# Phases of the convolution kernels as integers: a multiplication and two shifts instead of rounding and subtracting, integers read by ScalarE, and another order of the sums on TensorE

## The chip, the cores and the metric

The kernel runs on one core of a Trainium2 chip. The metric is device time in microseconds (us); the median of three runs of the kernel before is 2972.42 us (2969.39 to 2973.13). A profiled execution gives times of single instructions.

The engines are named as in the profile: PE (TensorE, matrix products; PEld its weight loads), DVE (VectorE, elementwise), ACT (ScalarE, functions such as exp and sin), POOL (GpSimd) and SP (which starts DMA transfers here). Each works off its own queue in order and waits at semaphores for the others. L431 means line 431 of the kernel.

## What is computed

Four layers on a sequence of 2048 positions and 640 channels: convolution layer, attention layer, and both again, each behind a layer norm and with a residual. Both convolution layers use the same kernel K, made from complex exponentials, which is what the change touches:

```python
def _A_ref(u, A_re, A_im, B_re, B_im, C_re, C_im, log_dt, Dskip):
    dt = jnp.exp(log_dt)[:, None]
    A = A_re + 1j * A_im
    ...
    logdA = dt * A
    dB = dt * Bc
    l = jnp.arange(L)
    P = jnp.exp(logdA[:, :, None] * l[None, None, :])
    K = jnp.einsum("dn,dnl,dn->dl", Cc, P, dB).real
    ...                       # y = causal convolution of u with K by FFT
    return y + u * Dskip

x = x + _A_ref(_layernorm(x), ...)
x = x + _B_ref(_layernorm(x), ...)    # attention, 32 query heads, one key/value head
x = x + _A_ref(_layernorm(x), ...)
x = x + _B_ref(_layernorm(x), ...)
```

For each of 640 channels d and 2048 positions l, K sums 128 complex exponentials. A position is split as l = 32 i + s with 64 values of i and 32 of s, so that an exponential is the product of one that depends on i and one that depends on s, and the sum over the 128 states is a small matrix product for each channel.

## The kernel before

The program runs in stages: generation of the kernels (`kgen`, up to about 300 us of the trace), spectra of the kernels, the first convolution layer, attention, the second convolution layer, attention. Only `_kgen` is touched.

`_kgen` first makes tables of three-part bf16 numbers (`ta`, `tb`, `tm`) from the parameters. Then 20 **units** of 32 channels each (16 channels times 2 parities) pass through a pipeline; a unit u needs:

- **phases**, two tiles h = 0, 1 of 128 x 1024. `phase_first(u, h)` has PE multiply a table by a constant grid `kg` into the PSUM tile `ph` (one buffer of two banks): the phase in turns, up to some sixteen of them. `phase(u, h)` has DVE take the fraction in [-0.5, 0.5]: `magic_round` (L241) rounds to whole turns into `r`, and L431 subtracts, into `f` (four buffers). Each reads `ph` from PSUM.
- **trig(u, h)** on ACT: Abs of `f` into `fa` (L444), sine of `f` (L445), cosine as sine of a quarter turn minus `fa` (L446). h = 0 gives C1 and S1, h = 1 gives C2 and S2. Two POOL memsets set the first column of C1 and S1.
- **sizes(u, k)** on PE, k = 0, 1, 2: the exponents of the magnitudes, into the PSUM tile `pe` with two buffers; **exps(u, k)** on ACT: exp of these (L462 for k = 0 and 1, into M1; L464 for k = 2, into M2).
- **products(u, k)** on DVE, k = 0, 1, 2, two operations each: magnitude by cosine into E1R (L472, L473), magnitude by sine in place into M1 (L476, L478), and C2 and S2 by M2 (L480, L481).
- **sums(u, ds)** on PE (L491): for each slice d of eight, small matmuls of E1R by C2 and M1 by S2 into the PSUM tile `pk`.
- **store(u)**: ACT copies `pk` out (L500) and SP stores it.

The order on PE, ACT and DVE is written out by hand (`manual_schedule`); the loop counts u from 0 to 22 and works on several units in one pass: in pass u the sizes, exponentials and trig of unit u, the phases of unit u + 1, the products of unit u - 1, the sums of unit u - 2, and the store of unit u - 3. Even and odd passes differ on ACT, so that sine and exp, which need different function tables, come in long runs: an even pass does both trigs and then the exponentials, an odd pass the exponentials and then both trigs. Passes 5 to 12 also hold the statistics of two tokens' tiles for the layer norm on DVE (L685, L687). Behind the last unit the weights of the transform (`wf`, L607) are loaded into space that the tables leave, and the spectra begin (L629).

The attention layers hold a DVE path, `power`, that is not touched: it turns scores from PSUM to int32 (L1356) and cuts the integers by bitwise operations (L1359, L1360).

Of the kernel before, what the change touches and what calls it, by code (L numbers as in the profile page):

```python
# [11 lines left out]
F32 = mybir.dt.float32  # L12
F32R = mybir.dt.float32r
BF16 = mybir.dt.bfloat16
I32 = mybir.dt.int32
AF = mybir.ActivationFunctionType
ALU = mybir.AluOpType
# [4 lines left out]
P = 128  # L22
# [6 lines left out]
TWO_PI = 2.0 * math.pi  # L29
# [170 lines left out]
class Net:  # L200
# [159 lines left out]
    def _kgen(self, ctx):  # L360
        tc, nc, ins = self.tc, self.nc, self.ins
# [33 lines left out]
        bp = ctx.enter_context(tc.tile_pool(name="kgb", bufs=2, reuse_waits="tile"))  # L395
# [1 line left out]

        units = [(q, r, q * 256 + 16 * r, 128, 128) for q in range(2) for r in range(8)]
        units += [(2, r, 512 + 16 * r, 64, 64) for r in range(4)]
        C1, S1, C2, S2, M1, M2, E1R, F, PH, PE_, PK, KST = ({} for _ in range(12))  # L400
        KST[0, 0] = bp.tile([P, 64, 32], F32, tag="kst", bufs=2, name="kst00")

        def big(tag, u, x, bufs=2):
            return bp.tile([P, 16, 2, x], F32, tag=tag, bufs=bufs, name=f"{tag}_{u}")

        def swap(a):
            return a.rearrange("p d a s -> p a d s")
# [8 lines left out]
        def phase_first(u, h):  # L416

            pp = PH[u, h] = kp.tile([P, 1024], F32, tag="ph", bufs=1, name=f"ph{u}{h}")
            src, col, rows = ((tb, 0, 48), (ta, 512, 96))[h]
            for par in range(2):  # L420
                nc.tensor.matmul(pp[:, 512 * par : 512 * par + 512], grp(src, u, par, rows),
                                 kg[0:rows, col : col + 512], start=True, stop=True)

        def phase(u, h):
            if (u, h) not in PH:
                phase_first(u, h)
            pp = PH.pop((u, h))
            r = bp.tile([P, 1024], BF16, tag="r", bufs=2, name=f"r{u}{h}")
            self.magic_round(r, pp)
            F[u, h] = bp.tile([P, 1024], F32, tag="f", bufs=4, name=f"f{u}{h}")  # L430
            nc.vector.tensor_tensor(F[u, h], pp, r, ALU.subtract)  # L431

        def trig(u, h):
            if h == 0:
                C1[u], S1[u] = big("c1", u, 33), big("s1", u, 33)
                nc.gpsimd.memset(C1[u][:, :, :, 0:1], 1.0)
                nc.gpsimd.memset(S1[u][:, :, :, 0:1], 0.0)
                s, c = swap(S1[u])[:, :, :, 1:33], swap(C1[u])[:, :, :, 1:33]
            else:
                C2[u], S2[u] = big("c2", u, 32, 3), big("s2", u, 32, 3)  # L440
                s, c = swap(S2[u]), swap(C2[u])
            f = F.pop((u, h))
            fa = bp.tile([P, 1024], F32, tag="fa", bufs=1, name=f"fa{u}{h}")
            nc.scalar.activation(fa, f, AF.Abs)  # L444
            nc.scalar.activation(s, f.rearrange("p (a d s) -> p a d s", a=2, d=16), AF.Sin, scale=TWO_PI)  # L445
            nc.scalar.activation(c, fa.rearrange("p (a d s) -> p a d s", a=2, d=16), AF.Sin,  # L446
                                 scale=-TWO_PI, bias=self.halfpi)

        def sizes(u, k):

# [15 lines left out]
        def products(u, k):  # L466

            tt = nc.vector.tensor_tensor
            if k == 0:
                E1R[u] = big("e1r", u, 64, 2)  # L470
                er, m1, c1 = (fl(a[u]) for a in (E1R, M1, C1))
                tt(er[:, :, 32:64], m1[:, :, 32:64], c1[:, :, 0:32], ALU.mult)  # L472
                tt(er[:, :, 0:32], m1[:, :, 0:32], c1[:, :, 32:0:-1], ALU.mult)  # L473
            elif k == 1:
                m1, s1 = (fl(a.pop(u)) for a in (dict(M1), S1))
                nc.vector.scalar_tensor_tensor(m1[:, :, 32:64], m1[:, :, 32:64], -1.0, s1[:, :, 0:32],  # L476
                                               op0=ALU.mult, op1=ALU.mult)
                tt(m1[:, :, 0:32], m1[:, :, 0:32], s1[:, :, 32:0:-1], ALU.mult)  # L478
            else:
                tt(C2[u], C2[u], M2[u], ALU.mult)  # L480
                tt(S2[u], S2[u], M2[u], ALU.mult)  # L481

        def sums(u, ds):

            if u not in PK:
                PK[u] = kp.tile([P, 512], F32, tag="pk", bufs=2, name=f"pk{u}")
            for d in ds:
                for e, c, first in ((E1R, C2, True), (M1, S2, False)):
                    for s in range(4):
                        dd, par = 8 * (s % 2) + d, s // 2  # L490
                        nc.tensor.matmul(PK[u][32 * s : 32 * s + 32, 64 * d : 64 * d + 64],  # L491
                                         c[u][:, dd, par], e[u][:, dd, par], start=first, stop=not first)

        def store(u):
            q, r, _, _, run = units[u]
            h, g = divmod(r, 4)
            if g == 0 and u > 0:
                KST[q, h] = bp.tile([P, 64, 32], F32, tag="kst", bufs=2, name=f"kst{q}{h}")
            kst = KST[q, h]
            nc.scalar.activation(kst[:, :, 8 * g : 8 * g + 8], PK[u].rearrange("p (d i) -> p i d", d=8), AF.Copy)  # L500
            if g == 3:
                for s in range(4):
                    par, dh = s // 2, s % 2
                    kd = self.kd[2 * q + par] if run == 128 else self.kd[4]
                    c0 = run // 2 * dh + 32 * h + (0 if run == 128 else 64 * par)
                    for jh in range(2):
                        dst = kd[64 * jh : 64 * jh + 64].rearrange("i (t d) -> t i d", d=DC)[:, :, c0 : c0 + 32]
                        nc.sync.dma_start(dst, kst[32 * s + 16 * jh : 32 * s + 16 * jh + 16])
            if r == 2 and q > 0:
                for c in (2 * q - 2, 2 * q - 1):  # L510
                    self.skip(c, self.kd[c, 0:1, 0:DC])
# [4 lines left out]
        with tc.manual_schedule(engines=engines):  # L516
            for h in range(2):
                phase(0, h)
            for u in range(n + 3):
                now, nxt, prod, tot = u < n, u + 1 < n, 0 < u <= n, 2 <= u < n + 2  # L520
                odd = u % 2 == 1
                if u >= 3:
                    store(u - 3)
                if now and not odd:
                    trig(u, 0)
                if prod:
                    products(u - 1, 0)
                if now:
                    sizes(u, 0)
                    if odd:  # L530
                        exps(u, 0)
                if nxt:
                    phase_first(u + 1, 0)
                if tot:
                    sums(u - 2, range(0, 2))
                if now:
                    sizes(u, 1)
                    if odd:
                        exps(u, 1)
                if tot:  # L540
                    sums(u - 2, range(2, 3))
                if nxt:
                    phase(u + 1, 0)
                if now and odd:
                    sizes(u, 2)
                    exps(u, 2)
                if prod:
                    products(u - 1, 1)
                if now:
                    trig(u, 0 if odd else 1)  # L550
                if tot:
                    sums(u - 2, range(3, 5))
                if nxt:
                    phase(u + 1, 1)
                if prod:
                    products(u - 1, 2)
                if tot:
                    sums(u - 2, range(5, 7))
                if now:
                    if odd:  # L560
                        trig(u, 1)
                    else:
                        exps(u, 0)
                        sizes(u, 2)
                        exps(u, 1)
                        exps(u, 2)
                if tot:
                    sums(u - 2, range(7, 8))
                if u == 0:
                    self.load_x()  # L570
                    nc.sync.dma_start(self.ident, ins["c_id"])
                if 5 <= u < 13:
                    self.stats(u - 5)
                for t in {n: range(8, 12), n + 1: range(12, 16)}.get(u, ()):
                    self.stats(t)
                if u == n:
                    early.close()
                    self.conv_weights(nc.sync)
# [1054 lines left out]
```

## Time and profile before

| | us |
|---|---|
| median of three runs | 2972.42 |
| lowest, highest | 2969.39, 2973.13 |
| profiled execution, whole | 2973.82 |
| its span, first to last instruction | 2971.8 |
| mean granted TensorE clock | 0.952 |

A row of a timeline gives the start in us from the span's start, the time in us, engine, line, operation, the tile written and those read, sizes, how many instructions are merged, and in brackets how long the engine sat idle before and what released it. A row of the groups gives line, engine, operation, shapes and count, then the busy time in us and the mean of one in ns, then idle time before them and its releasers. Consecutive DVE and ACT instructions overlap a little in their records, so the distance from start to start is the better measure of what one costs in a sequence.

### The profile page before, as it was taken

The page shows a single profiled execution, that of the slowest core. Times are in us where ns is not written, and L with a number is a line of the kernel's source. Part 1 is how long each engine was busy: PE and PEld are TensorE (multiplying, and loading weights), DVE is VectorE, ACT ScalarE, POOL GpSimd, SP SyncE. Part 2 cuts the span into 40 slices and gives each one's busy share as a digit, 9 for nine tenths or more (in the row PEclk, how much of TensorE's full clock was granted, in tenths as well). Part 3 has the DMA queues.
Part 4 walks back from the last instruction along what each step waited for, and adds up shares of the span by engine and source line. Part 5 has one row for each costly group of instructions (what it writes and reads, how often), then busy time and mean ns, then how long its engine had stood idle before and what let it go on. Part 6 is the DMA issues. An engine that isn't in the chain of part 4 may idle for free. (4 is left out here: it accounts for less than half of the span.)

```text
span 2971.8 us, 71403 instructions
## 1 busy us (share of the span) xinstructions
PE 2720.8 (92%) x29916; PEld 1563.3 (53%) x29916; DVE 2375.0 (80%) x2820; ACT 2397.1 (81%) x3065; POOL 293.1 (10%) x514
## 2 busy tenths in 40 slices
PE   2776989898899999999999999898999999999999
PEld 0333978775344444444444688773444444444444
DVE  7999899943678888888888699826788888878885
ACT  5888243444899999999999734337999999999997
POOL 0000001100201011010101011001111110101101
PEclk9655999998999999999999999898999999999999
DMA  6113555533211111111111255231111211211211
GB/s 146 35 17 99 172 183 114 119 122 104 84 36 33 35 33 36 35 35 37 31 36 34 92 114 126 87 127 54 34 34 35 55 33 37 51 35 33 54 32 31
DMA packets 156101, 196.30 MB, mean 66 GB/s; under 512 B 66221, under 2 KB 123533, under 8 KB 152149
## 3 DMA queue, kind: packets, MB, share of 16 engines
q1 hardware_dynamic: 119704, 141.90, 16.2%
q0 software_dynamic: 33776, 48.08, 8.0%
q8 instruction: 239, 3.92, 0.5%
q10 hardware_dynamic: 2288, 1.64, 0.2%
q14 instruction: 94, 0.76, 0.1%
HBM read 111.47 MB, written 48.55 MB: 54 GB/s over the span
## 5 line engine op out<-in xcount | busy, mean ns | idle before, releaser
L1346 ACT ACTIVATE pw<-pw 128x1024 f32<-128x1024 f32 (+3 forms) x840 | 765.6, 957 | 0.0
L1323 ACT ACTIVATE pt<-scb 128x1024 f32<-128x1024 f32 x684 | 699.3, 1133 | 23.2 <-PE scb L1313 21.5
L1323 ACT ACTIVATE pt<-scd 128x1024 f32<-128x1024 f32 x684 | 703.8, 1148 | 11.7 <-PE scd L1313 5.6
L1338 DVE COPY pw<-scd 128x1024 f32<-128x1024 f32 x307 | 375.2, 1222 | 81.6 <-PE scd L1313 65.5
L1338 DVE COPY pw<-scb 128x1024 f32<-128x1024 f32 x307 | 374.7, 1221 | 79.8 <-PE scb L1313 64.1
L1313 PE MATMUL scb<-qpb,kt 62*128 62x512 f32 x2048 | 367.4, 446 | 29.3 <-DVE pw L1338 13.6
L1313 PE MATMUL scd<-qpd,kt 62*128 62x512 f32 x2048 | 366.5, 445 | 19.8 <-ACT pt L1323 7.5
L1377 PE MATMUL pob<-pt,vt 128*32 128x256 f32 x5472 | 368.1, 387 | 0.0
L1377 PE MATMUL pod<-pt,vt 128*32 128x256 f32 x5472 | 367.6, 386 | 0.0
L1313 PEld LDWEIGHTS scb<-qpb,kt 62*128 62x128 f32 x2048 | 169.8, 186 | 252.8 <-ACT pt L1323 146.8
L1313 PEld LDWEIGHTS scd<-qpd,kt 62*128 62x128 f32 x2048 | 169.0, 186 | 245.0 <-ACT pt L1323 154.6
L1363 DVE SCALAR_TENSOR_TENSOR zh<-zh,zm 128x1024 f32<-128x1024 f32 x198 | 239.7, 1210 | 0.0
L1377 PEld LDWEIGHTS pob<-pt,vt 128*32 128x32 f32 x5472 | 143.3, 109 | 166.8 <-issue 108.0
L1377 PEld LDWEIGHTS pod<-pt,vt 128*32 128x32 f32 x5472 | 143.3, 109 | 164.6 <-issue 105.8
L1377 PE MATMUL pob<-pw,vt 128*32 128x256 f32 x2456 | 164.8, 381 | 0.4 <-ACT pw L1346 0.4
L1377 PE MATMUL pod<-pw,vt 128*32 128x256 f32 x2456 | 163.9, 379 | 0.4 <-ACT pw L1346 0.4
L1409 POOL DMA_DIRECT2D dn<-on x62 | 43.6, 703 | 1192.7 <-DVE on L1408 1155.6
L1415 POOL DMA_DIRECT2D rc<-ivd x248 | 125.8, 513 | 115.4 <-DMA ivd<-dn 111.6
L1446 DVE TENSOR_TENSOR x<-pyd,x 128x320 f32<-128x320 f32 x147 | 71.7, 488 | 77.9 <-PE pyd L1459 77.8
L1446 DVE TENSOR_TENSOR x<-pyb,x 128x320 f32<-128x320 f32 x147 | 71.7, 488 | 77.1 <-PE pyb L1459 77.0
L1459 PE MATMUL pyb<-wo,ot 128*32 128x320 f32 x1176 | 106.7, 434 | 5.3 <-DVE on L1408 4.5
L1459 PE MATMUL pyd<-wo,ot 128*32 128x320 f32 x1176 | 106.7, 434 | 4.4 <-DVE on L1408 3.6
(391 smaller groups left out, 4139.8 us busy)
## 6 DMA issues: line engine op xcount, KB each, us to landing
Akh<-kh SPq DMA_DIRECT2D x10, 2048.0 KB
rc<-ivd POOLq DMA_DIRECT2D x248, 64.0 KB, 2.2
kh<-Ak SPq DMA_DIRECT2D x5, 2048.0 KB
qhd<-qh SPq DMA_DIRECT2D x40, 256.0 KB
qld<-ql SPq DMA_DIRECT2D x40, 256.0 KB
qpb<-qhd SPq DMA_DIRECT2D x256, 40.0 KB
qpd<-qhd SPq DMA_DIRECT2D x256, 40.0 KB
ot<-on SPq DMA_DIRECT2D x216, 40.0 KB
```

The costliest lines, as they stand in the source:

```text
L1313: nc.tensor.matmul(sc[:, 512 * par : 512 * par + 512], kt[rows, 128 * t : 128 * t + 128], qps[nb, hg][rows, f].rearrange("p a c -> p (a c) ...
L1323: nc.scalar.activation(pt, sc, AF.Exp, scale=SCALE)
L1338: nc.vector.tensor_copy(cols, sc)
L1346: nc.scalar.activation(cols, cols, AF.Exp, scale=SCALE)
L1363: nc.vector.scalar_tensor_tensor(h, a, c[k], f, op0=ALU.add, op1=ALU.mult)
L1377: nc.tensor.matmul(po[32 * j : 32 * j + 32, 256 * f : 256 * f + 256], v[:, t], pt[j], start=(t == 0), stop=(t == 15))
L1409: nc.gpsimd.dma_start(den, on[20:128:32].rearrange("j (c r) -> j c r", c=32))
L1415: nc.gpsimd.dma_start(inv[32 * j : 32 * j + 32], self.ivd[hg % 2, j : j + 1].to_broadcast([32, 512]))
L1446: nc.vector.tensor_tensor(xh, py, xh, ALU.add)
L1459: nc.tensor.matmul(py[j : j + m], o[:, 128 * i + j : 128 * i + j + m], w[:, c0 : c0 + n], start=start, stop=stop)
```

## The change

`phase` is split into `turns` and `fraction`. `turns` multiplies the phase by 2^23 and writes int32 (tile `z`, one buffer, in place of `r`): the low 23 bits are the fraction of a turn. `fraction` shifts left by 9 and arithmetically right by 9, so that these bits become a signed integer in [-2^22, 2^22); it reads and writes SBUF. `f` is now int32. ACT reads that in Abs and sine, and the scales of both sines are divided by 2^23. In the loop the sums of unit u - 2 are distributed differently: before, slices 0 and 1 stood ahead of sizes(u, 1), slice 2 behind it, slices 3 and 4 ahead of the second phase, 5 and 6 behind it, and slice 7 at the end of the pass; now none stands ahead of sizes(u, 1), and the rest depends on whether the pass is even or odd.

```diff
-        def phase(u, h):
+        def turns(u, h):
+
             if (u, h) not in PH:
                 phase_first(u, h)
             pp = PH.pop((u, h))
-            r = bp.tile([P, 1024], BF16, tag="r", bufs=2, name=f"r{u}{h}")
-            self.magic_round(r, pp)
-            F[u, h] = bp.tile([P, 1024], F32, tag="f", bufs=4, name=f"f{u}{h}")
-            nc.vector.tensor_tensor(F[u, h], pp, r, ALU.subtract)
+            Z[u, h] = bp.tile([P, 1024], I32, tag="z", bufs=1, name=f"z{u}{h}")
+            nc.vector.tensor_scalar(Z[u, h], pp, 2.0**23, None, ALU.mult)
+
+        def fraction(u, h):
+
+            f = bp.tile([P, 1024], I32, tag="f", bufs=4, name=f"f{u}{h}")
+            nc.vector.tensor_scalar(f, Z.pop((u, h)), 9, 9, ALU.logical_shift_left, ALU.arith_shift_right)
+            F[u, h] = f
+
+        def phase(u, h):
+            turns(u, h)
+            fraction(u, h)
...
             nc.scalar.activation(fa, f, AF.Abs)
-            nc.scalar.activation(s, f.rearrange("p (a d s) -> p a d s", a=2, d=16), AF.Sin, scale=TWO_PI)
+            nc.scalar.activation(s, f.rearrange("p (a d s) -> p a d s", a=2, d=16), AF.Sin,
+                                 scale=TWO_PI / 2.0**23)
             nc.scalar.activation(c, fa.rearrange("p (a d s) -> p a d s", a=2, d=16), AF.Sin,
-                                 scale=-TWO_PI, bias=self.halfpi)
+                                 scale=-TWO_PI / 2.0**23, bias=self.halfpi)
...
                 if nxt:
                     phase_first(u + 1, 0)
-                if tot:
-                    sums(u - 2, range(0, 2))
                 if now:
                     sizes(u, 1)
                     if odd:
                         exps(u, 1)
                 if tot:
-                    sums(u - 2, range(2, 3))
+                    sums(u - 2, range(0, 1) if odd else range(0, 4))
                 if nxt:
                     phase(u + 1, 0)
                 if now and odd:
...
                 if tot:
-                    sums(u - 2, range(3, 5))
+                    sums(u - 2, range(1, 5) if odd else range(4, 7))
                 if nxt:
                     phase(u + 1, 1)
                 if prod:
                     products(u - 1, 2)
                 if tot:
-                    sums(u - 2, range(5, 7))
+                    sums(u - 2, range(5, 8) if odd else range(7, 8))
                 if now:
                     if odd:
                         trig(u, 1)
...
                         exps(u, 2)
-                if tot:
-                    sums(u - 2, range(7, 8))
```

More of the change, by code (lines that the diff above doesn't have):

```diff
@@ L399, in _kgen @@
         units += [(2, r, 512 + 16 * r, 64, 64) for r in range(4)]
-        C1, S1, C2, S2, M1, M2, E1R, F, PH, PE_, PK, KST = ({} for _ in range(12))
+        C1, S1, C2, S2, M1, M2, E1R, F, FA, Z, PH, PE_, PK, KST = ({} for _ in range(14))
         KST[0, 0] = bp.tile([P, 64, 32], F32, tag="kst", bufs=2, name="kst00")
```

## The prediction

> **What bounds the kernel now.** I read the page first, then the groups by shape up to 420 us, the windows, and the timelines of DVE, ACT and PE. The change touches only the generation of the convolution kernels, a loop over 20 units (u = 0 to 19) between about 44 and 300 us; the rest of the program keeps its instructions. The page's first line is an average over stages and says little here:
>
> ```profile
> PE 2720.8 (92%) x29916; PEld 1563.3 (53%) x29916; DVE 2375.0 (80%) x2820; ACT 2397.1 (81%) x3065; POOL 293.1 (10%) x514
> ```
>
> A window inside the loop (busy time of PE, PEld, DVE, ACT, POOL; granted clock; DMA) looks as if DVE alone were the bound:
>
> ```profile
> 135.00:160.00 25.00, 17.76 (x293) 8.14 (x292) 24.73 (x27) 21.96 (x23) 0.63 (x4) 0.57 0.01 1
> ```
>
> But DVE works off a queue, and whether it sets the pace shows only where somebody waits for it. So I read ACT, whose order repeats every two units: even u does trig, trig, three exponentials; odd u three exponentials, trig, trig. Its timeline, from one odd unit's first Abs (u=7) to the next (u=9), and the first and last odd unit:
>
> ```profile
> 65.06 1.05 ACT L444 ACTIVATE fa<-f 128x1024 f32<-128x1024 f32 x1
> ...
> 137.83 1.05 ACT L444 ACTIVATE fa<-f 128x1024 f32<-128x1024 f32 x1
> ...
> 153.23 1.94 ACT L462 ACTIVATE m<-pe 128x1024 f32<-128x1024 f32 x2
> 155.36 1.02 ACT L464 ACTIVATE m<-pe 128x1024 f32<-128x1024 f32 x1 [0.19 <-PE pe L454]
> ...
> 156.91 1.02 ACT L462 ACTIVATE m<-pe 128x1024 f32<-128x1024 f32 x1
> 159.73 1.02 ACT L462 ACTIVATE m<-pe 128x1024 f32<-128x1024 f32 x1 [1.80 <-PE pe L454]
> 161.28 1.02 ACT L464 ACTIVATE m<-pe 128x1024 f32<-128x1024 f32 x1 [0.53 <-PE pe L454]
> 162.20 1.05 ACT L444 ACTIVATE fa<-f 128x1024 f32<-128x1024 f32 x1
> ...
> 284.58 1.05 ACT L444 ACTIVATE fa<-f 128x1024 f32<-128x1024 f32 x1
> ```
>
> This pair takes 162.20 - 137.83 = 24.37 us, of which ACT waits 0.19 + 1.80 + 0.53 = 2.52 for PE's sizes: **ACT's own work is 21.85 us a pair**. Over nine pairs the mean is (284.58 - 65.06) / 9 = 24.39. PE is what ACT waits for; DVE's own pace comes next:
>
> ```profile
> 145.57 1.21 DVE L472 TENSOR_TENSOR e1r<-m,c 128x1024 f32<-128x1024 f32 x1
> ...
> 158.27 1.21 DVE L472 TENSOR_TENSOR e1r<-m,c 128x1024 f32<-128x1024 f32 x1
> ...
> 255.39 1.22 DVE L472 TENSOR_TENSOR e1r<-m,c 128x1024 f32<-128x1024 f32 x1
> ...
> 257.67 1.22 DVE L241 TENSOR_SCALAR r<-ph 128x1024 bf16<-128x1024 f32 x1
> 258.92 1.22 DVE L431 TENSOR_TENSOR f<-ph,r 128x1024 f32<-128x1024 f32 x1
> 260.06 1.22 DVE L476 SCALAR_TENSOR_TENSOR m<-m,s 128x1024 f32<-128x1024 f32 x1
> ...
> 266.99 1.22 DVE L472 TENSOR_TENSOR e1r<-m,c 128x1024 f32<-128x1024 f32 x1
> ```
>
> A unit takes DVE 266.99 - 255.39 = 11.60 us, and 158.27 - 145.57 = 12.70 with the layer's statistics (u = 5 to 12, so 8 of 18 units). Two units are 23.20 plain, 25.40 with them, on average 24.2. **Two limits lie on top of each other**: DVE at 24.2 and the ACT-PE round at 24.37. Lifting one alone gives next to nothing; the change touches both.
>
> **The change part by part.** *DVE.* Both steps of a phase go from 1.22 us each (40 of each) to a product with integer output and a double shift from SBUF:
>
> ```profile
> L431 DVE TENSOR_TENSOR f<-ph,r 128x1024 f32<-128x1024 f32 x40 | 49.0, 1225 | 2.0
> L241 DVE TENSOR_SCALAR r<-ph 128x1024 bf16<-128x1024 f32 x40 | 48.7, 1218 | 7.7 <-PE ph L421 7.4 <-DMA hdare<-hare 0.3
> ```
>
> The attention's power path holds operations of the same form, PSUM to int32 and then int32 to int32 with two bitwise operations:
>
> ```profile
> 740.67 1.23 DVE L1356 TENSOR_SCALAR z<-scb 128x1024 int32<-128x1024 f32 x1 [1.12 <-PE scb L1313]
> 741.93 0.69 DVE L1359 TENSOR_SCALAR zm<-z 128x1024 int32<-128x1024 int32 x1
> 742.66 0.69 DVE L1360 TENSOR_SCALAR z<-z 128x1024 int32<-128x1024 int32 x1
> 743.27 1.22 DVE L1338 COPY pw<-scb 128x1024 f32<-128x1024 f32 x1
> ```
>
> From start to start the product takes 1.26 and the bitwise step 743.27 - 742.66 = 0.61: 1.87 against (260.06 - 257.67) = 2.39 now. That is 0.52 a phase, four phases a pair: **2.08 us a pair**, so DVE needs 21.1 plain, 23.3 with statistics, 22.1 on average. No row has shifts: they cost between 0.61 (as the bitwise rows) and 1.14 (a full-rate step, no gain); I take 0.61, the same instruction with another operator on the same types. Besides, the bank of the phase (one buffer) comes free after the first operation, not the second, 1.1 us sooner for PE.
>
> *PE.* The sums now stand behind sizes(u,1) and, in odd units, only one of their eight slices stands ahead of sizes(u,2). Around u=8 and u=9:
>
> ```profile
> 154.31 1.01 PE L454 MATMUL pe<-kg,tm 96*128 96x512 bf16 x2 [1.89 <-ACT m L462]
> 155.25 0.44 PE L491 MATMUL pk<-e1r,c 128*32 128x64 f32 x8
> ...
> 155.84 1.03 PE L454 MATMUL pe<-kg,tm 48*128 48x512 bf16 x2
> 156.67 1.06 PE L421 MATMUL ph<-kg,tb 48*128 48x512 bf16 x2
> 157.65 0.44 PE L491 MATMUL pk<-e1r,c 128*32 128x64 f32 x8
> ...
> 158.67 1.03 PE L454 MATMUL pe<-kg,tm 48*128 48x512 bf16 x2
> ```
>
> Steps: 0.94 for a sizes ahead of sums, 0.59 for one slice with its change-over, 0.83 and 0.98 for sizes and phase, 1.03 until a result is there. From the same anchor, 154.31 (sizes(8,2), freed by an exponential): slice 7 now lies ahead, where PE waits 1.89 anyway, so it costs nothing. sizes(9,0) at 155.25, the phase of unit 10 at 156.08, sizes(9,1) at 157.06, ready 158.09, so that exponential starts at 158.1 instead of 159.73, after a wait of 0.17 instead of 1.80. One slice (from 158.02), sizes(9,2) at 158.61, ready 159.64: the next starts at 159.68 instead of 161.28 and waits 0.56. The following Abs comes at 160.60 instead of 162.20: **a pair takes 22.77**, 21.85 of work and 0.92 of waits. In the last pair no next phase stands ahead of sizes(19,1): in the same times it starts when its buffer comes free (155.36 + 1.02 = 156.38), is ready 157.41 and nobody waits; sizes(19,2) starts at 157.93, when the exponential ahead has freed its buffer, is ready 158.96, and the Abs comes at 159.90: 22.07.
>
> What the moved slices hold up: behind 158.61 PE has, until sizes(10,2) can start again at 154.31 + 22.77 = 177.08, a size (0.94), fifteen slices (0.43 each, from 1.02 - 0.16 for two), three phases (0.98) and two more sizes: 12.2 us of work in 18.5. So **6.3 us of slack** cover the later sums; if that cover went, each us would go into ACT's wait.
>
> *ACT* reads int32 instead of f32 in 80 instructions:
>
> ```profile
> L445 ACT ACTIVATE s<-f 128x1024 f32<-128x1024 f32 x40 | 42.2, 1056 | 0.1
> L444 ACT ACTIVATE fa<-f 128x1024 f32<-128x1024 f32 x40 | 42.1, 1052 | 6.0 <-DVE f L431 5.3
> ```
>
> No row has ACT reading an integer. The nearest are these and the 1.02 from PSUM: a source in another memory changes 0.03. Bounds are -0.03 and +1.05 (twice the time); I take nothing, since DVE's z with int32 output (1.23) costs what its bf16 r (1.22) does. The scale only changes its value.
>
> *Start.* Ahead of unit 1 ACT waits for PE, and PE for the phase's bank:
>
> ```profile
> 55.04 1.23 DVE L241 TENSOR_SCALAR r<-ph 128x1024 bf16<-128x1024 f32 x1 [5.03 <-PE ph L421]
> ...
> 57.67 1.01 PE L421 MATMUL ph<-kg,ta 96*128 96x512 bf16 x2 [1.81 <-DVE f L431]
> ...
> 59.57 1.02 ACT L464 ACTIVATE m<-pe 128x1024 f32<-128x1024 f32 x1 [2.33 <-PE pe L454]
> ```
>
> With the bank free at 55.04 + 1.23 the phase starts at 56.3, 1.4 sooner, and the same one unit on: Abs of unit 1 near 62.9 instead of 65.06, 2.2 gained.
>
> *End.* What follows the last trig hangs on it in one chain:
>
> ```profile
> 283.65 5.16 SPq L607 DMA_DIRECT2D wf<-in_c_wf  x8
> ...
> 289.15 1.23 DVE L472 TENSOR_TENSOR e1r<-m,c 128x1024 f32<-128x1024 f32 x1 [3.16 <-ACT c L446]
> ...
> 299.47 1.27 PE L629 MATMUL zk<-Rk,wf 128*128 128x128 f32 x9
> ```
>
> DVE waits 3.16 for ACT, six products, the last sums, then the first spectrum. The load of wf goes out when the last sizes have been read and moves along. So the stage's gain is the program's.
>
> **Sum.** Nine pairs: 8 x 22.77 + 22.07 = 204.2 against 219.5, 15.3 gained; the start 2.2; together 17.5 of the profiled execution's 2973.82 us (span 2971.8): 2956.3. That execution is 1.4 above the median of the runs shown, 2972.42; from that it would be 2954.9. I take **2956**. DVE's 22.1 lies under 22.77; it falls behind only in the statistics' units, by 23.3 - 22.77 = 0.5 a pair and 2 us in all, and what PE waits for from it (phase banks, products) has the 6.3 us of slack. The one buffer of the integer tile costs nothing: its next writer comes behind its reader on the same engine.
>
> **Rivals.** *PE goes to full clock.* The same sizes took 0.60 in a stretch of full clock:
>
> ```profile
> 262.82 0.60 PE L454 MATMUL pe<-kg,tm 48*128 48x512 bf16 x2
> ```
>
> With that the 0.92 of waits goes and DVE's 22.1 is the bound: 9 x 0.67 = 6 more, 2950. Against it: from 154.31 on PE ran without a gap for 5 us and the sizes started at 158.67 still took 1.03. The Trainium skill, "TensorE: Matmul & The Clock Gate", What's actually happening, says that a busy window of about 3.4 us brings the full clock; by that rule the longer unbroken stretch after the change gives this rival's 2950, and the trace, slow through 5 us of work, does not bear it out.
>
> *Only part arrives:* moved sums delay PE's phases and ACT's waits stay near 2 us a pair, so 23.8: 9 x 0.59 + 2.2 = 7.5 gained, 2966. For it: one buffer of the phase ties PE to DVE. Against: the 6.3 us.
>
> *The shifts run at full rate.* DVE stays at 24.2 a pair and ACT follows it: the start's 2.2 and at most 0.19 a pair, 2971. Against: the 0.69 rows.
>
> *Slower: ACT reads int32 slowly.* The place is L444 and L445, 80 instructions on the engine that is then the bound. It decides from 17.5 / 80 = 0.22 us each; at the upper bound, 1.05, it costs 84 and gives 2956 + 84 = 3040. Against: nothing in the rows ties ACT's time to a type.
>
> **How the numbers follow.** Forecast 0.66 (2949 to 2963 by its terms: waits between none and 1.5 a pair), full clock 0.10, part 0.13, shifts at full rate 0.06, slow integers 0.05. The range 2947 to 2968 leaves out the last two and the rims. What can be told from no change here is about 0.2%, 6 us. Faster by more: 0.66 + 0.10 + 0.09 of the part = 0.85; within: 0.04 + 0.06 = 0.10; slower 0.05.
>
> **What would show it.** The shift near 0.69 us, ACT's Abs and Sin still near 1.05, ACT's wait for L454 near 0.9 a pair, odd Abs 22.8 apart, the first spectrum's matmul near 282, and the same lengths behind it. Wrong: shifts of 1.2, Abs well over 1.05, DVE e1r waited for in every pair, or pairs still over 24.

## The result and the profile after

The changed kernel takes 2952.99 us (median of four runs, 2949.65 to 2953.52) against 2971.95 us for the kernel before (four runs, 2969.39 to 2973.13): a ratio of 0.9932, 95% interval 0.992 to 0.9944. That is 19 us less; 2956 was forecast, with 2947 to 2968 as the range. The profiled execution took 2953.42 us, its span 2951.7.

The groups by shape of the changed kernel up to 400 us show what the replaced operations and their readers now cost:

```profile
L430 DVE TENSOR_SCALAR z<-ph 128x1024 int32<-128x1024 f32 x40 | 48.7, 1218 | 9.6 <-PE ph L421 9.3 <-DMA hdare<-hare 0.3
...
L454 ACT ACTIVATE s<-f 128x1024 f32<-128x1024 int32 x40 | 42.2, 1056 | 0.1
L453 ACT ACTIVATE fa<-f 128x1024 f32<-128x1024 int32 x40 | 42.1, 1053 | 5.4 <-DVE f L435 4.8
...
L435 DVE TENSOR_SCALAR f<-z 128x1024 int32<-128x1024 int32 x40 | 27.9, 696 | 2.0
```

The product costs what the rounding cost (1218 ns, both), the double shift 696 ns where the subtraction took 1225, and ACT reads integers in the time of floats (1053 and 1056 ns against 1052 and 1056).

ACT's timeline in the changed kernel: the first and the last odd unit's Abs, and one pair between two of them.

```profile
63.03 1.05 ACT L453 ACTIVATE fa<-f 128x1024 f32<-128x1024 int32 x1
...
130.68 1.05 ACT L453 ACTIVATE fa<-f 128x1024 f32<-128x1024 int32 x1
...
148.19 1.02 ACT L474 ACTIVATE m<-pe 128x1024 f32<-128x1024 f32 x1 [0.18 <-PE pe L464]
...
150.86 1.02 ACT L472 ACTIVATE m<-pe 128x1024 f32<-128x1024 f32 x1 [0.24 <-PE pe L464]
152.41 1.02 ACT L474 ACTIVATE m<-pe 128x1024 f32<-128x1024 f32 x1 [0.53 <-PE pe L464]
153.33 1.05 ACT L453 ACTIVATE fa<-f 128x1024 f32<-128x1024 int32 x1
...
266.09 1.05 ACT L453 ACTIVATE fa<-f 128x1024 f32<-128x1024 int32 x1
```

The pair takes 153.33 - 130.68 = 22.65 us, and ACT's waits in it are 0.18 + 0.24 + 0.53 = 0.95; without them 21.70, nearly the 21.85 from before. From the first to the last odd Abs are 203.06 us, against 219.52. PE's side of the same pair, from the size that an exponential frees:

```profile
147.14 1.97 PE L464 MATMUL pe<-kg,tm 96*128 96x512 bf16 x4 [3.71 <-ACT m L472]
148.91 1.06 PE L421 MATMUL ph<-kg,tb 48*128 48x512 bf16 x2
149.76 1.06 PE L464 MATMUL pe<-kg,tm 48*128 48x512 bf16 x2
150.75 0.44 PE L501 MATMUL pk<-e1r,c 128*32 128x64 f32 x8
...
151.34 1.03 PE L464 MATMUL pe<-kg,tm 96*128 96x512 bf16 x2
```

Two sizes, a phase, a size, one slice of the sums, a size: the order that the diff wrote out. The 0.53 of ACT's wait is the slice between the last two. The spectra begin at 280.99 instead of 299.47:

```profile
280.99 1.65 PE L635 MATMUL zk<-Rk,wf 128*128 128x128 f32 x12
```

So 18.5 of the 20.1 us between the two spans were won in the loop and its start. The remaining 1.6 lie behind it, where the kernels are alike; nothing was run to find them, and the four runs of either kernel differ by 3.7 us and more among themselves.

### The profile page after: what moved, and what is told of

It reads as the page before. It is cut to its first block, busy times and chain, and to the rows that moved or that the text cites. A ratio compares the mean times of both kernels' runs of the same rounds, so it can differ in the third digit from the quotient of the medians.

```text
span 2951.7 us, 71427 instructions
## 1 busy us (share of the span) xinstructions
PE 2699.0 (91%) x29916; PEld 1564.1 (53%) x29916; DVE 2354.8 (80%) x2820; ACT 2395.4 (81%) x3065; POOL 294.0 (10%) x514
## 5 line engine op out<-in xcount | busy, mean ns | idle before, releaser
L1329 ACT ACTIVATE pt<-scb 128x1024 f32<-128x1024 f32 x684 | 699.2, 1133 | 23.3 <-PE scb L1319 17.0
```

The costliest lines, as they stand in the source:

```text
L1329: nc.scalar.activation(pt, sc, AF.Exp, scale=SCALE)
```

## Experiments

**The two halves alone.** The first keeps the old arithmetic and takes the new order of the sums, the second the reverse.

The order alone, against the changed kernel (the scales of the sines as before too):

```diff
-            Z[u, h] = bp.tile([P, 1024], I32, tag="z", bufs=1, name=f"z{u}{h}")
-            nc.vector.tensor_scalar(Z[u, h], pp, 2.0**23, None, ALU.mult)
...
+            r = bp.tile([P, 1024], BF16, tag="r", bufs=2, name=f"r{u}{h}")
+            self.magic_round(r, pp)
+            F[u, h] = bp.tile([P, 1024], F32, tag="f", bufs=4, name=f"f{u}{h}")
+            nc.vector.tensor_tensor(F[u, h], pp, r, ALU.subtract)
```

The shifts alone, against the changed kernel (all slices of the sums where they stood before):

```diff
                 if nxt:
                     phase_first(u + 1, 0)
+                if tot:
+                    sums(u - 2, range(0, 2))
                 if now:
                     sizes(u, 1)
...
-                    sums(u - 2, range(0, 1) if odd else range(0, 4))
+                    sums(u - 2, range(2, 3))
...
-                    sums(u - 2, range(1, 5) if odd else range(4, 7))
+                    sums(u - 2, range(3, 5))
...
-                    sums(u - 2, range(5, 8) if odd else range(7, 8))
+                    sums(u - 2, range(5, 7))
...
+                if tot:
+                    sums(u - 2, range(7, 8))
```

> The new order of the sums with the old rounding and subtraction. Theory (two limits on top of each other): ACT's waits for PE's sizes fall, but DVE keeps its 23.2 us for a plain pair of units and 25.4 with statistics, 24.2 on average, so the odd units' Abs stay 24.0 to 24.4 apart on average and the time is 2969 to 2973 us. Rival (the order does it all): pairs of 22.8 us and 2955 to 2958 us.

> The integer phases with the old order of the sums. Theory: ACT goes on waiting some 1.8 and 0.5 us a pair for PE's sizes, pairs stay at 24.4 us; gained are the start's 2 us and the 1.4 us by which two pairs with statistics exceeded 24.4: 2967 to 2971 us. Rival (DVE's time does it all): pairs near 22.7 us and 2953 to 2957 us.

The order alone takes 2969.18 us against 2972.37 (ratio 0.9988, interval 0.9979 to 0.9998), the shifts alone 2967.36 (0.9982, 0.9973 to 0.9992): 3.2 and 5.0 us. Together they bring 19, far more than the sum of the two, 8.2. Neither rival holds. With the order alone, ACT's timeline in units with statistics shows who sets the pace:

```profile
134.61 1.05 ACT L444 ACTIVATE fa<-f 128x1024 f32<-128x1024 f32 x1
...
153.18 1.02 ACT L465 ACTIVATE m<-pe 128x1024 f32<-128x1024 f32 x1 [1.23 <-PE pe L455]
...
157.21 1.02 ACT L463 ACTIVATE m<-pe 128x1024 f32<-128x1024 f32 x1 [1.60 <-PE pe L455]
158.99 1.02 ACT L465 ACTIVATE m<-pe 128x1024 f32<-128x1024 f32 x1 [0.76 <-PE pe L455]
159.91 1.05 ACT L444 ACTIVATE fa<-f 128x1024 f32<-128x1024 f32 x1
```

159.91 - 134.61 = 25.30 us is DVE's demand for a pair with statistics, 25.4. The waits still name PE, though the slices are out of the way: PE itself is late, since a phase ahead of the size waits for DVE.

```profile
155.29 1.03 PE L421 MATMUL ph<-kg,tb 48*128 48x512 bf16 x2 [1.18 <-DVE f L431]
156.12 1.06 PE L455 MATMUL pe<-kg,tm 48*128 48x512 bf16 x2
```

The size begun at 156.12 is ready at 157.18, and ACT's exponential starts at 157.21. In the second run ACT's old waits are there unchanged, 1.80 and 0.53:

```profile
157.21 1.02 ACT L472 ACTIVATE m<-pe 128x1024 f32<-128x1024 f32 x1 [1.80 <-PE pe L464]
158.76 1.02 ACT L474 ACTIVATE m<-pe 128x1024 f32<-128x1024 f32 x1 [0.53 <-PE pe L464]
159.68 1.05 ACT L453 ACTIVATE fa<-f 128x1024 f32<-128x1024 int32 x1
...
184.04 1.05 ACT L453 ACTIVATE fa<-f 128x1024 f32<-128x1024 int32 x1
```

The pair is 24.36, and so is every pair but the first and the last, those with statistics too: DVE has room (busy 23.57 of 25 us from 135 to 160 us, with statistics), and ACT and PE hold each other at the old round.

**Giving DVE's time back.** The next run puts a double shift by zero behind each fraction, with the order and the early release of the phase's bank as in the changed kernel.

```diff
             nc.vector.tensor_scalar(f, Z.pop((u, h)), 9, 9, ALU.logical_shift_left, ALU.arith_shift_right)
+            nc.vector.tensor_scalar(f, f, 0, 0, ALU.logical_shift_left, ALU.arith_shift_right)
             F[u, h] = f
```

> The changed kernel with a second double shift, by zero, behind each fraction: 0.61 us more on DVE a phase, 2.44 us a pair, with order and early release of the phase's bank kept. Theory: DVE needs 23.5 us plain and 25.8 us with statistics a pair, 24.5 on average, and sets the pace: 2968 to 2974 us, so nearly the whole gain goes. Rival (DVE has slack, PE's order is what counts): 2953 to 2957 us.

2974.39 us against 2972.37 (ratio 1.0007, 0.9997 to 1.0016): the whole gain goes, just above the stated 2968 to 2974. DVE's timeline tells why it is a little more:

```profile
143.04 0.69 DVE L435 TENSOR_SCALAR f<-z 128x1024 int32<-128x1024 int32 x1
143.77 0.69 DVE L436 TENSOR_SCALAR f<-f 128x1024 int32<-128x1024 int32 x1
144.38 1.22 DVE L491 TENSOR_TENSOR c<-c,m 128x1024 f32<-128x1024 f32 x1
```

Behind an operation whose result it reads, the second one starts 0.73 us later, not 0.61; four a pair make 2.9 where 2.44 were reckoned, and more than the 2.08 that the change had saved. So time on DVE, and not only the earlier release of the bank, carries the gain.

**How far ACT's wait can be taken down.** In the changed kernel the 0.53 is slice 0 of the sums; the next run moves it behind sizes(u,2). The changed kernel ran beside it.

```diff
-                if tot:
-                    sums(u - 2, range(0, 1) if odd else range(0, 4))
+                if tot and not odd:
+                    sums(u - 2, range(0, 4))
...
-                    sums(u - 2, range(1, 5) if odd else range(4, 7))
+                    sums(u - 2, range(0, 5) if odd else range(4, 7))
```

> The changed kernel itself, beside the three below on the same chip: 2950 to 2954 us.

> In odd units slice 0 of the sums goes behind sizes(u,2) too. Theory (ACT with its waits for PE is the bound): the wait of 0.53 us goes, a pair takes 22.1 instead of 22.65 us, just at DVE's average of 22.1: 3 to 5 us less than the changed kernel, 2947 to 2950 us. Rival (DVE, busy 24.7 of 25 us, is the bound already): no change, 2951 to 2954 us.

2947.66 us against 2951.65 of the changed kernel beside it, 4.0 less (ratio to the kernel before 0.9919, 0.9906 to 0.9933; the changed kernel 0.9932, 0.9918 to 0.9945). Run again it took 2946.79. The wait is gone, and the pair is 150.80 - 128.71 = 22.09:

```profile
128.71 1.05 ACT L453 ACTIVATE fa<-f 128x1024 f32<-128x1024 int32 x1
...
148.91 1.02 ACT L472 ACTIVATE m<-pe 128x1024 f32<-128x1024 f32 x1 [0.24 <-PE pe L464]
149.88 1.02 ACT L474 ACTIVATE m<-pe 128x1024 f32<-128x1024 f32 x1
150.80 1.05 ACT L453 ACTIVATE fa<-f 128x1024 f32<-128x1024 int32 x1
```

The rival, that DVE with 24.7 busy us in 25 is the bound already, falls: 4 us went without touching DVE's work. This is the fastest complete kernel of the study.

**The limit behind it.** The changed kernel without the second Abs of each unit, whose second cosines are then those of half the angle, so that it computes another K:

```diff
-            fa = bp.tile([P, 1024], F32, tag="fa", bufs=1, name=f"fa{u}{h}")
-            nc.scalar.activation(fa, f, AF.Abs)
+            if h == 0:
+                fa = bp.tile([P, 1024], F32, tag="fa", bufs=1, name=f"fa{u}{h}")
+                nc.scalar.activation(fa, f, AF.Abs)
+            else:
+                fa = f
...
-                                 scale=-TWO_PI / 2.0**23, bias=self.halfpi)
+                                 scale=-TWO_PI / 2.0**(23 + h), bias=self.halfpi)
```

> The changed kernel without the Abs of the second phase tile of each unit; its cosines are of half the angle. ACT has 1.92 us less a pair. Theory: DVE's 22.1 us a pair is the next limit, so only 0.5 us a pair is gained: 2947 to 2951 us. Rival (ACT alone is the bound): 1.9 us a pair, 17 us, 2934 to 2938 us.

2945.65 us, 6.0 under the changed kernel, where ACT alone as the bound would have given 17. ACT's timeline shows DVE's own pace, undisguised:

```profile
104.16 1.05 ACT L454 ACTIVATE fa<-f 128x1024 f32<-128x1024 int32 x1
...
126.32 1.05 ACT L454 ACTIVATE fa<-f 128x1024 f32<-128x1024 int32 x1
...
149.52 1.05 ACT L454 ACTIVATE fa<-f 128x1024 f32<-128x1024 int32 x1
...
172.72 1.05 ACT L454 ACTIVATE fa<-f 128x1024 f32<-128x1024 int32 x1
...
239.29 1.05 ACT L454 ACTIVATE fa<-f 128x1024 f32<-128x1024 int32 x1
...
260.42 1.05 ACT L454 ACTIVATE fa<-f 128x1024 f32<-128x1024 int32 x1
```

The two pairs from 126.32 to 172.72 take 23.20 us each, DVE's reckoned 23.3 with statistics; the last of the loop, without them, takes 21.13, its 21.1. The time lies 1.35 us below the expected range. Of the nine pairs only the first is clearly shorter than DVE's demand, by 1.0 (20.10 against 21.1); why was not looked into.

**A phase moved into PE's idle time.** PE waits 3.71 us ahead of sizes(u,2) in even units. This run starts from the one with slice 0 moved and puts the next unit's phase there.

```diff
-                if nxt:
+                if nxt and (u + 1, 0) not in PH:
                     phase_first(u + 1, 0)
...
+                        if u + 2 < n:
+                            phase_first(u + 2, 0)
                         exps(u, 0)
                         sizes(u, 2)
```

> As the one before, and the first phase that PE makes in an odd unit is made at the end of the even unit ahead, before sizes(u,2), where PE waits 3.7 us for ACT. Theory: the wait of 0.24 us goes too, ACT could do 22.0 us a pair, but DVE's 22.1 us holds: 0 to 2 us less than the one before, 2946 to 2949 us. Rival (PE now waits for the phase's bank there and delays sizes(u,2)): 1 us or more above the one before.

2950.76 us, 3.1 above the run before it: the theory fell. At the start, PE and ACT:

```profile
58.49 1.01 PE L421 MATMUL ph<-kg,tb 48*128 48x512 bf16 x2 [1.31 <-DVE z L430]
59.43 4.12 PE L464 MATMUL pe<-kg,tm 96*128 96x512 bf16 x8
```

```profile
60.51 1.02 ACT L474 ACTIVATE m<-pe 128x1024 f32<-128x1024 f32 x1 [3.74 <-PE pe L464]
```

The size of unit 0 now stands behind a phase that waits for DVE; the first odd Abs comes at 64.51 instead of 62.81. To see whether that is all, the first unit got its old place back:

```diff
-                        if u + 2 < n:
+                        if 0 < u < n - 2:
                             phase_first(u + 2, 0)
```

> As e5, but the first unit's pass keeps the old place of that phase, so that sizes(0,2) does not stand behind the phase of unit 2. Theory (e5 lost 1.7 us there, and with it the lead that carries DVE through the pairs with statistics): the odd units' first Abs comes near 62.8 us again, plain pairs take 22.0 us, and the time is 0 to 2 us below e4_again. Rival (the phase ahead of sizes(u,2) costs in every pair): 2 to 4 us above e4_again as e5 was.

> The kernel with slice 0 behind sizes(u,2), again beside e7 on one chip: 2946 to 2949 us.

2948.01 us (2947.62 to 2949.64) against 2946.79 (2945.28 to 2948.03): 1.2 above, not 0 to 2 below, so the new theory held for part only. The runs of the two overlap, so the traces have to say where it is lost. In the units with statistics:

```profile
167.97 1.01 PE L421 MATMUL ph<-kg,tb 48*128 48x512 bf16 x2 [2.54 <-DVE z L430]
168.92 3.15 PE L464 MATMUL pe<-kg,tm 96*128 96x512 bf16 x6
```

```profile
169.99 1.02 ACT L474 ACTIVATE m<-pe 128x1024 f32<-128x1024 f32 x1 [1.41 <-PE pe L464]
```

Once DVE lags there, the phase keeps PE waiting for DVE and the size behind it keeps ACT waiting for PE, 1.41 us: three pairs took 22.87, 23.20 and 23.28 us, near DVE's pace with statistics, where the order without this move let ACT run on at 22.07 to 22.09 in the same three while DVE fell behind. The plain pairs took 21.97, as expected. A queue that PE works off in order turns a lag that nobody needed to notice into a wait.

## Why the prediction was right

- *Two limits on top of each other*: shown. 3.2 and 5.0 us alone, 19 together. "Next to nothing" was a little strong: each half also gains the start or some pairs, as with the shifts alone, where the two pairs over 24.4 us disappear.
- *DVE*: 0.61 was taken for the shift's step and 2.08 us a pair, so 21.1 and 23.3. The step is 142.43 - 141.82 = 0.61 in the changed kernel, and the run without one Abs showed pairs of 21.13 and 23.20. The rival of shifts at full rate fell with the 696 ns.

```profile
140.57 1.22 DVE L430 TENSOR_SCALAR z<-ph 128x1024 int32<-128x1024 f32 x1
141.82 0.69 DVE L435 TENSOR_SCALAR f<-z 128x1024 int32<-128x1024 int32 x1
142.43 1.22 DVE L486 SCALAR_TENSOR_TENSOR m<-m,s 128x1024 f32<-128x1024 f32 x1
```

- *PE's walk from 154.31*: waits of 0.92 and a pair of 22.77 were forecast; 0.95 and 22.65 came. The missing 0.12 lies almost whole in one step of the walk. From a phase to the size behind it the prediction took 0.98, which is the step from a phase to the sums; it is 149.76 - 148.91 = 0.85. (At the start of the loop before the change, where a size follows a phase too, it is 0.80 to 0.86.) The last pair takes 22.1, as forecast (22.07).
- *ACT's own work*: 21.85 was read, 21.70 came, though ACT does the same. The 21.85 held a wait that the profile does not mark. Before the change the exponential at 156.91 started 0.63 us after a store's copy (first row below), when the size begun at 155.84 had just become ready (155.84 + 1.03 = 156.87). After the change the same step is 0.48 (the other two rows). So ACT's waits were 2.67 a pair where the prediction read 2.52. The forecast pair does not hang on that division, since it was reckoned from PE's times.

```profile
156.28 0.59 ACT L500 ACTIVATE kst<-pk 128x512 f32<-128x512 f32 x1
```

```profile
149.11 0.59 ACT L510 ACTIVATE kst<-pk 128x512 f32<-128x512 f32 x1
149.59 1.03 ACT L472 ACTIVATE m<-pe 128x1024 f32<-128x1024 f32 x1
```

- *ACT reads integers*: no cost, as taken; the rival that ended slower fell with 1053 ns.
- *Start*: 62.9 forecast, 63.03 came; the second profile of the changed kernel has 62.32.
- *End*: the first spectrum near 282 forecast, 280.99 came. From the last odd Abs to it are 14.90 us, before 14.89, so the stage's gain was the program's.
- *The sum*: 17.5 was reckoned, the loop and start gave 18.5. The first pair took 22.33 instead of 22.77, and the next seven 0.1 less each. The forecast of 2956 starts from the profiled execution before; from the median of its runs the same sum gives 2954.9, 1.9 above what came.
- *The slack of PE* (6.3 us for the later sums): nothing that ACT waits for became later, and moving one more slice back still gained 4.0 us. From the size at 151.34 to the one at 169.80, which an exponential frees, PE stood idle for 7.07 us (1.18 + 0.60 + 0.69 + 1.44 + 3.16), the last 3.16 waiting for ACT. How many more slices that would take without a new wait was not tried.
- *Full clock*: in part. PE's granted clock is 0.72 from 110 to 135 us and 0.62 from 135 to 160 us, where it was 0.57 in both, and 0.57 to 0.65 in each 25 us from 160 to 260 us, where it was 0.50; only from 60 to 85 us it fell, from 1.00 to 0.83. But the fully clocked stretches don't fall where ACT waits:

```profile
154.17 0.91 PE L421 MATMUL ph<-kg,ta 96*128 96x512 bf16 x2
155.01 0.32 PE L501 MATMUL pk<-e1r,c 128*32 128x64 f32 x8
...
155.82 0.60 PE L464 MATMUL pe<-kg,tm 48*128 48x512 bf16 x2
```

The granted clock is 0.50 up to 154 us and 1.00 from 155 us on, nearly 8 us into a stretch without a gap that began at 147.14; the sizes that ACT waits for lie in its first 5.2 us, at 1.03. The Trainium skill, "TensorE: Matmul & The Clock Gate", What's actually happening, has a sustained busy window of about 3.4 us bring the full clock. The traces agree with it only in part. From 60 us on, the clock came up in the loop 8.3 to 9.5 us into such a stretch in all four cases of the kernel before, and 6.4 to 9.2 us into one in nine cases of the changed kernel; in the stretch of some 8 us from 154.31 of the kernel before it did not come up. In three more cases of the changed kernel (at 117, 209 and 254 us) it came up within 3.1 us of PE's last gap. So the length of the unbroken stretch alone doesn't settle it; why was not tried.

## What to carry to other kernels

An engine that is busy all the time is not therefore the bound: look at the period of the engine whose order repeats, take its waits out, and compare the demands of all engines per period. Where two lie within a per cent (24.2 and 24.4 us here), a change to either alone looks nearly worthless (3.2 and 5.0 us here, 19 together), and both have to be lifted in one go. In a queue that is worked off in order, put first what another engine waits for, and ahead of it nothing that waits for a third.

## What was not expected of the hardware

A double shift that reads the result of the 0.69 us shift directly ahead of it starts 0.73 us after that one, where an independent operation follows after 0.61: 0.12 us for this link of a chain. Operations of 1.22 us show nearly the same in the prediction's rows: the subtraction starts 258.92 - 257.67 = 1.25 us after the rounding whose result it reads, and the independent operation behind it after 260.06 - 258.92 = 1.14. The step of 0.73 already stands in the prediction's rows of the attention's bitwise operations (742.66 - 741.93); there the second overwrites what the first reads.
